# A soft-capped attention with a gated convolution behind it: the order of every engine's work written down in new tables

## The chip, the cores and the metric

The kernel runs on one core of one Trainium2 chip. A core has engines with a queue each: TensorE (PE, matrix products; its weight loads are PEld), VectorE (DVE), ScalarE (ACT), GpSimd (POOL) and SyncE (SP), which here issues all DMAs. Every queue is in order: an instruction that waits holds up all that stand behind it on its engine. The metric is the time of one execution on the device in microseconds (us), the median of several runs; less is better.

## What is computed

```python
def _attn_ref(q, k, v, cap):                       # 8 batches, 12 heads, 448 rows, 64 columns, float32
    scores = np.matmul(q, k.transpose(0, 1, 3, 2)) / np.sqrt(q.shape[-1])
    scores = cap * np.tanh(scores / cap)           # cap = 30
    attn = np.exp(scores - np.max(scores, axis=-1, keepdims=True))
    attn = attn / (np.sum(attn, axis=-1, keepdims=True) + 1e-09)
    return np.matmul(attn, v)

def _moe_ref(x, w_val, conv_w, w_out):             # x: 8 x 448 x 768, the heads side by side
    gate_pre = causal_conv(x, conv_w)              # 5 taps along the rows, each column by itself
    gate = 1.0 / (1.0 + np.exp(-gate_pre))
    return gate * (x @ w_val) @ w_out              # both weights 768 x 768
```

The weights w_val, w_out and conv_w come as float64.

## The kernel before

**Tiles.** The work is cut into 48 *pairs* p: two heads of one batch, which fill 128 partitions. Six pairs make a batch, called a *block* b (0 to 7). Everything is held turned, with a head's columns on the partitions.

For a pair, the steps are, with the lines of the profile: `load_q`, `load_k` (L186), `load_v` (L198): DMAs. `tq`, `tk` (L305): VectorE transposes q and k. `scores` (p, i), i = 0 to 3 (L326): TensorE makes scores of 112 keys against 448 queries for both heads, into a PSUM tile `pss` of which there are two; for pairs 0 to 12 in plain fp32, from pair 13 on in three products of high and low halves, which `q_hi`, `k_hi` (ScalarE, L311) and `q_lo`, `k_lo` (VectorE, L240) make. `tanh` (L334) and `exp` (L338): ScalarE, one tile of 112 x 896 each, into `pt`, of which there are six. `add` (VectorE, L345, L348): for pairs 6 to 10 the four `pt` are added in twos, from pair 11 on to one. `av` (p, i) (L363): TensorE, the product with v, into the one `psa`. `sums` (L375): TensorE, the row sums by a product with ones, into the one `psz`; four rounds for pairs 0 to 5, two up to 10, then one. `turn_sums`, `recip`, `spread`, `mul` (VectorE, L383 to L404): the division, which leaves x in one of two buffers `u`. `x_hi` (ScalarE, L409), `x_lo` (VectorE, L240): the halves of x. `conv` (p, 0 to 4) (L421 to L425): the five taps, on VectorE; for p < 11 the first one on ScalarE.

For a block and each of its six groups d of 128 columns: `sigmoid` (ScalarE, L431), `val` (TensorE, L446 to L448, two halves of nine matmuls, each half over three pairs' x), `gate` (VectorE, L452), `gated_hi` (ScalarE, L455), `gated_lo` (VectorE). Then `out_part` (TensorE, L475 to L477, six or eight tiles m, two halves of nine matmuls each), `store` (ScalarE copies the tile, L483) and `store_out` (DMA, L487); `keep_tail` (GpSimd, L462) carries rows over to the next block. val and out share two PSUM tiles `psf`. In twelve steps the weights are split into halves: `weight_load`, `late_load` (DMA), `weight_first` (ScalarE, L140, L141), `weight_second`, `weight_third` (VectorE).

**Order.** Nothing is ordered by a scheduler. Each step gets a number, "when", in units of pairs: p plus an entry of a table. The list of all steps is sorted by it, and each engine's queue holds its steps in that order:

```python
with tc.manual_schedule(engines={ENG.Activation, ENG.PE, ENG.DVE, ENG.Pool, ENG.SP}):
    for _, _, f, a in sorted(events, key=lambda e: e[:2]):
        f(*a)
```

The numbers are no times: an engine runs its next step as soon as what it needs is there. Before, the tables hold one row for a kind of pair (`EARLY` for pairs 0 to 5, `PAIRED`, `STEADY`, `SPLIT`, with changes like `TOGETHER` or `GATE_FIRST` by p % 6), so that the order repeats from block to block. For pair 25 it gives:

```
TensorE  scores25.0 scores25.1 av24.0-3 sums24 val3.1 (2 halves) scores25.2 scores25.3 val3.2 scores26.0 scores26.1 av25.0-3 sums25
ScalarE  tanh25.0 tanh25.1 exp25.0 exp25.1 q_hi26 k_hi26 sigmoid3.0-5 x_hi24 tanh25.2 gated_hi3.0 gated_hi3.1 tanh25.3 exp25.2 exp25.3
VectorE  add25.0 q_lo26 k_lo26 gate3.0 gate3.1 gated_lo3.0 gated_lo3.1 x_lo24 conv24.0-4 gate3.2 add25.1 add25.2
```

and for pair 27 `x_lo26 conv26.0-4 add27.1 add27.2` on VectorE. All six sigmoids of a block stand together.

Of the kernel before, what the change touches and what calls it, by code (L numbers as in the profile page):

```python
# [40 lines left out]
STEADY = {  # L41
    "load_q": -1.9,
    "load_k": -1.85,
    "load_v": -0.6,
    "tq": -0.90,
    "tk": -0.85,
    "scores": (0.0, 0.05, 0.62, 0.67),
    "tanh": (0.06, 0.13, 0.68, 0.75),
    "exp": (0.22, 0.29, 0.82, 0.89),
    "add": (0.52, 1.03, 1.06),  # L50
    "av": (1.10, 1.15, 1.20, 1.25),
    "sums": (1.28,),
    "turn_sums": 1.41,
    "recip": 1.42,
    "spread": 1.44,
    "mul": 1.50,
    "x_hi": 1.52,
    "x_lo": 1.58,
    "conv": (1.60, 1.61, 1.64, 1.67, 1.70),
}  # L60

SPLIT = STEADY | {"q_hi": -0.69, "k_hi": -0.68, "q_lo": -0.475, "k_lo": -0.47}
PAIRED = STEADY | {"add": (0.52, 1.03), "sums": (1.28, 1.29)}
EARLY = {
    "load_q": -1.9,
    "load_k": -1.85,
    "load_v": -0.7,
    "tq": -0.72,
    "tk": -0.70,
    "scores": (-0.50, -0.49, 0.10, 0.11),  # L70
    "tanh": (0.0, 0.01, 0.35, 0.36),
    "exp": (0.17, 0.18, 0.52, 0.53),
    "av": (0.28, 0.37, 0.65, 0.80),
    "sums": (0.29, 0.38, 0.66, 0.81),
    "turn_sums": 1.02,
    "recip": 1.03,
    "spread": 1.04,
    "mul": 1.05,
    "x_hi": 1.30,
    "x_lo": 1.34,  # L80
    "conv": (1.31, 1.50, 1.52, 1.54, 1.56),
}

SIXTH = PAIRED | {k: EARLY[k] for k in ("tq", "tk", "scores", "tanh", "exp")} | {"add": (0.38, 0.62)}


TOGETHER = {
    "scores": (0.0, 0.05, 0.31, 0.32),
    "tanh": (0.06, 0.13, 0.34, 0.36),
    "exp": (0.22, 0.29, 0.47, 0.53),  # L90
    "add": (0.52, 0.60, 0.61),
}
NEXT_TOGETHER = {
    "turn_sums": 1.41, "recip": 1.42, "spread": 1.43, "mul": 1.44, "x_hi": 1.45, "x_lo": 1.54,
    "conv": (1.58, 2.16, 2.17, 2.18, 2.19),
}
PREPARE_TOGETHER = {"q_hi": -0.69, "k_hi": -0.68, "q_lo": -0.44, "k_lo": -0.43}

GATE_FIRST = {"x_lo": 1.66, "conv": (1.67, 1.68, 1.69, 1.70, 1.71)}
LATE_X = {"x_lo": 1.76, "conv": (1.78, 1.80, 1.83, 1.86, 1.89)}  # L100
NEARLY, NPAIRED, NPLAIN = 6, 11, 13

VAL_FIRST = (6.50, 6.85, 7.36, 7.74, 8.36, 8.74)
VAL = (6.85, 7.36, 7.74, 8.36, 8.74, 9.36)
SIG_FIRST, SIG_AT = 6.92, 7.44
OUT_EVEN = (9.80, 10.36, 10.74, 11.36, 11.74, 12.36)
OUT_ODD = (9.80, 10.36, 10.74, 10.80, 11.36, 11.74, 11.80, 12.36)
OUT_LATE = (9.80, 10.36, 10.74, 11.74, 12.36, 12.60)
PART = 0.13
KEEP_AT = 10.2  # L110
W_AT = (0.70, 1.70, 2.70, 3.70, 4.70, 5.70, 7.1, 8.035, 9.035, 9.7, 10.4, 11.035)
W_LOAD = -0.5
W_SECOND, W_THIRD, W_THIRD_EARLY = 0.02, 0.05, 0.71
W_FREE = 11.3
CW_LOAD, CW_AT = -0.55, 0.6
EPS = 1e-9
# [13 lines left out]
def float64_split(nc, raw, mid, hi, lo, t):  # L130

    tf = t.bitcast(F32)
    top = raw[..., 1].bitcast(F32)

    def first():
        nc.scalar.activation(tf, top, AF.Copy, scale=2.0 ** -112)  # L140
        nc.scalar.sign(top, top)  # L141
# [60 lines left out]
def fast_path(tc, io, u2, q, k, v, w_val, conv_w, w_out, out, capt):  # L202
# [22 lines left out]
    with ExitStack() as ctx:  # L225
# [37 lines left out]
        wstate = {}  # L263
# [11 lines left out]
        def late_load(n):  # L275
# [5 lines left out]
            wstate[n] = wstate[n], shifted(late, NH)  # L281

        def weight_first(n):
            _, c, nh, w = wsteps[n]
            t = wsc.tile([P, WC, NH], I32, name="w_t")
            wstate[n] = float64_split(nc, *wstate[n], w[:, c, nh, 0], w[:, c, nh, 1], t)
# [63 lines left out]
        def bank(p, name):  # L350

            if p < NEARLY and p % 2:
# [3 lines left out]
        def attnv(p, i):  # L356
# [5 lines left out]
            for j, r in enumerate(ROWS):  # L362
                nc.tensor.matmul(  # L363
                    st["o"][r, :S], vloads[p][:, j, i], t[:, j], start=(i == 0), stop=(i == NKT - 1)
                )

        def sums(p, i):

            st = state[p]
            n = len(tables[p]["sums"])  # L370
# [5 lines left out]
            if i == n - 1:  # L376
                vloads.pop(p)
# [29 lines left out]
        def x_hi(p):  # L407
            xh = wk.tile([P, S], F32R, name="xh", bufs=NXX)
            nc.scalar.copy(xh, gates[p][1][:, PAD:PAD + S])  # L409
# [80 lines left out]
        cw_steps = []  # L490
        events = []
        tables = [EARLY if p < NEARLY else SIXTH if p == NEARLY else PAIRED if p < NPAIRED else STEADY if p < NPLAIN else SPLIT for p in range(NP)]
        for p in range(NPAIRED, NP):
            if p % NPAIR == 0:
                tables[p] = tables[p] | LATE_X

        def together(p):
            return NPLAIN < p < NP and p % NPAIR not in (1, 3)

        for p in range(NPLAIN, NP):  # L500
            if together(p - 1):
                tables[p] = tables[p] | PREPARE_TOGETHER
            if together(p):
                tables[p] = tables[p] | TOGETHER
            if p % NPAIR == 2:
                tables[p] = tables[p] | GATE_FIRST
            if together(p + 1):
                tables[p] = tables[p] | NEXT_TOGETHER

# [13 lines left out]
        for p, table in enumerate(tables):  # L523
            for name, f in steps.items():
                x = table.get(name, ())
                if isinstance(x, tuple):
                    for i, y in enumerate(x):
                        at(p + y, f, p, i)
                else:
                    at(p + x, f, p)  # L530
        for b in range(B):
            t0 = NPAIR * b
            for d in range(NCC):
                sig = SIG_AT if b else SIG_FIRST
                y = (VAL if b else VAL_FIRST)[d]
                at(t0 + sig, sigmoid, b, d)
                for i in range(PARTS):
                    at(t0 + y + i * PART, val, b, d, i)
                done = t0 + max(y + PARTS * PART, sig + 0.17)
                at(done + 0.01, gate, b, d)  # L540

                last = d == NCC - 1
                at(done + (0.02 if last else 0.08), gated_hi, b, d)
                at(done + (0.03 if last else 0.12), gated_lo, b, d)
            if b % 2 == 0:
                at(t0 + KEEP_AT, keep_tail)
            for m, y in enumerate(OUT_ODD if b % 2 else OUT_LATE if b == B - 2 else OUT_EVEN):
                for i in range(PARTS):
                    at(t0 + y + i * PART / 2, out_part, b, m, i)
                at(t0 + y + 0.20, store, b, m)  # L550
                at(t0 + y + 0.40, store_out, b, m)
        for n, t0 in enumerate(W_AT):
            third = [x + (W_THIRD if x > NEARLY else W_THIRD_EARLY) for x in W_AT]
# [186 lines left out]
```

## Time and profile before

| | |
|---|---|
| median of 3 runs | 743.75 us (742.98 to 746.29) |
| span of the profiled execution, first to last instruction | 739.6 us |
| TensorE busy | 717.1 us, 97% |
| VectorE busy | 593.0 us, 80% |
| ScalarE busy | 534.7 us, 72% |
| GpSimd busy | 9.0 us, 1% |
| moved by DMA | 63.75 MB |

The profile is of one execution of its own. Busy is the time in which at least one instruction of the engine ran. A row of a timeline is: start, duration, engine, line, operation, tile written <- tiles read, form, count, and in brackets the engine's idle time just before and what ended it. A row of waits is: who waited for whom, total us, times, longest. The end of a matmul is modelled, so that the records of two in a row overlap.

### The profile page before, as it was taken

Reading aid. Unit: us, or ns where it says so; the run is one execution under the profiler, and the core shown is the slowest. Engines: PE = TensorE matmul, PEld = TensorE weight load, DVE = VectorE, ACT = ScalarE, POOL = GpSimd, SP = SyncE. Lnnn points to the kernel's source line nnn. Section 1 sums busy time; section 2 is a strip of 40 time slices with the busy share of each in tenths; the row PEclk is TensorE's granted clock in tenths of the full one; section 3 lists DMA queues with packets and bytes.
Section 4 is the critical chain, followed back from the end, with each engine's and each line's share of the span. In section 5 each row is a group of like instructions: output and inputs, shape, how many; then the busy total and the mean of one; then the engine's idle time right before and its main releaser. Section 6 shows DMA issues by size and latency. Waiting matters only on the chain.

```text
span 739.6 us, 10858 instructions
## 1 busy us (share of the span) xinstructions
PE 717.1 (97%) x3972; PEld 488.8 (66%) x3972; DVE 593.0 (80%) x972; ACT 534.7 (72%) x708; POOL 9.0 (1%) x16
## 2 busy tenths in 40 slices
PE   5999999999999999999999999999999999999997
PEld 2333655556767776686677766757766876676997
DVE  2899999888997789988899669988899778997410
ACT  5899977787876678776957679587787659774311
POOL 0000001000000000000000000000000000000000
PEclk9999999999999999999999999999999999999999
DMA  6998867854223332224331333223322333200001
GB/s 109 223 212 209 202 171 154 225 118 80 39 49 80 74 74 38 61 67 88 57 57 47 88 75 65 39 69 74 73 38 61 70 87 57 51 24 33 23 22 68
DMA packets 241820, 63.75 MB, mean 86 GB/s; under 512 B 228448, under 2 KB 235616, under 8 KB 241760
## 3 DMA queue, kind: packets, MB, share of 16 engines
q1 hardware_dynamic: 241760, 62.98, 38.6%
q8 instruction: 33, 0.54, 0.3%
q14 instruction: 27, 0.22, 0.1%
HBM read 51.94 MB, written 11.01 MB: 85 GB/s over the span
## 4 chain that ended last, share of the span: by engine, by line
PE 52%; DVE 21%; ACT 13%; issue 2%; SPq 1%; DMA 0%; DVEq 0%; ACTq 0%
PE pss L326 9%; PE psf L475 8%; PE psf L477 7%; PE psf L476 7%; DVE gate L425 7%; PE psa L363 6%; PE psf L446 4%; PE psf L447 4%; PE psf L448 4%; ACT pt L334 3%; PE psz L375 3%; DVE pa L348 3%; ACT gate L431 3%; ACT pt L338 2%; DVE pa L345 2%
## 5 line engine op out<-in xcount | busy, mean ns | idle before, releaser
L334 ACT ACTIVATE pt<-pss,rc 112x896 f32<-112x896 f32 x192 | 185.1, 1004 | 39.2 <-PE pss L326 39.2
L338 ACT ACTIVATE pt<-pt,capt 112x896 f32<-112x896 f32 x192 | 189.6, 1041 | 0.1
L363 PE MATMUL psa<-pt,vn 112*64 112x448 f32 x720 | 147.7, 546 | 0.0
L425 DVE SCALAR_TENSOR_TENSOR gate<-u,cw,gate 128x448 f32<-128x448 f32 x192 | 130.6, 680 | 5.7
L475 PE MATMUL psf<-wo,g_h 128*128 128x384 f32 x336 | 115.7, 344 | 0.0
L477 PE MATMUL psf<-wo,g_l 128*128 128x384 f32 x336 | 112.6, 335 | 0.0
L476 PE MATMUL psf<-wo,g_h 128*128 128x384 f32 x336 | 112.4, 335 | 0.0
L446 PE MATMUL psf<-xh,wv 128*128 128x448 f32 x288 | 107.5, 373 | 0.1
L448 PE MATMUL psf<-xl,wv 128*128 128x448 f32 x288 | 104.5, 363 | 0.0
L447 PE MATMUL psf<-xh,wv 128*128 128x448 f32 x288 | 104.4, 362 | 0.0
L363 PEld LDWEIGHTS psa<-pt,vn 112*64 112x64 f32 x720 | 47.8, 136 | 81.4 <-issue 69.7
L348 DVE TENSOR_TENSOR pa<-pt 112x896 f32<-112x896 f32 x84 | 91.1, 1085 | 2.8 <-ACT pt L338 2.8
L483 ACT COPY osb<-psf 128x384 f32<-128x384 f32 x56 | 26.6, 475 | 65.3 <-PE psf L477 63.6
L383 DVE STREAM_TRANSPOSE zt<-psz 128x448 f32<-128x448 f32 x45 | 28.8, 640 | 54.2 <-PE psz L375 54.2
L475 PEld LDWEIGHTS psf<-wo,g_h 128*128 128x128 f32 x336 | 63.1, 188 | 12.3 <-issue 11.3
L446 PEld LDWEIGHTS psf<-xh,wv 128*128 128x128 f32 x288 | 54.0, 187 | 20.2 <-issue 5.4
L476 PEld LDWEIGHTS psf<-wo,g_h 128*128 128x128 f32 x336 | 63.1, 188 | 0.0
L477 PEld LDWEIGHTS psf<-wo,g_l 128*128 128x128 f32 x336 | 63.1, 188 | 0.0
L326 PE MATMUL pss<-qt,kt 64*112 64x448 f32 x208 | 49.6, 594 | 12.3 <-DVE guard L249 7.8
L455 ACT CAST g_h<-gate 128x448 fp32r<-128x448 f32 x48 | 26.3, 562 | 47.2 <-DVE gate L452 47.0
L326 PE MATMUL pss<-qh,kh 64*112 64x448 f32 x280 | 58.0, 408 | 0.0
L409 ACT CAST xh<-u 128x448 fp32r<-128x448 f32 x48 | 27.1, 566 | 42.3 <-DVE u L404 42.0
(74 smaller groups left out, 908.6 us busy)
## 6 DMA issues: line engine op xcount, KB each, us to landing
vn<-in_v_dram SPq DMA_DIRECT2D x96, 112.0 KB, 2.6
out_dram<-osb SPq DMA_DIRECT2D x56, 192.0 KB, 1.9
qn<-in_q_dram SPq DMA_DIRECT2D x188, 56.0 KB, 2.5
kn<-in_k_dram SPq DMA_DIRECT2D x188, 56.0 KB, 2.4
w_raw<-in_moe_w_val_dram SPq DMA_DIRECT2D x12, 384.0 KB, 5.1
w_late<-in_moe_w_val_dram SPq DMA_DIRECT2D x12, 384.0 KB, 4.4
w_raw<-in_moe_w_out_dram SPq DMA_DIRECT2D x12, 384.0 KB, 3.8
w_late<-in_moe_w_out_dram SPq DMA_DIRECT2D x12, 384.0 KB, 4.8
```

Of the source, the lines that this page charges most:

```text
L326: nc.tensor.matmul(ps[:CH, j, :S], st[x][r, c], st[y][r], start=(n == 0), stop=(n == len(parts) - 1))
L334: nc.scalar.activation(st["p", i], st.pop(("s", i)), AF.Tanh, scale=rc8[:CH])
L338: nc.scalar.activation(t, t, AF.Exp, scale=capt[:CH])
L348: nc.vector.tensor_tensor(st["a", i], st["p", 2 * i], st["p", 2 * i + 1], op=ALU.add)
L363: nc.tensor.matmul(st["o"][r, :S], vloads[p][:, j, i], t[:, j], start=(i == 0), stop=(i == NKT - 1))
L425: nc.vector.scalar_tensor_tensor(g, u[:, i:i + S], cw[:, hp, i:i + 1], g, ALU.mult, ALU.add)
L446: nc.tensor.matmul(o, w_h, xh, start=(c == 0), stop=False)
L447: nc.tensor.matmul(o, w_l, xh, start=False, stop=False)
L448: nc.tensor.matmul(o, w_h, xl, start=False, stop=(c == NCC - 1))
L475: nc.tensor.matmul(o, g_h[:, d, s], w_h, start=(d == 0), stop=False)
L476: nc.tensor.matmul(o, g_h[:, d, s], w_l, start=False, stop=False)
L477: nc.tensor.matmul(o, g_l[:, d, s], w_h, start=False, stop=(d == NCC - 1))
```

## The change

The rows by kind of pair give way to explicit tables: `PAIRS` with a row of its own for every pair (41 entries, one for each step in the order of `STEPS`, "-" where a pair has no such step), `BLOCKS` with a row for every block (for each d: sigmoid, two halves of val, gate, gated_hi, gated_lo; for each m: two halves of out_part, store, store_out; then keep_tail) and `WEIGHTS` with a row for every weight step. Every entry is its own number. The tiles, buffers, shapes and the number of rounds of sums and adds stay.

```diff
-STEADY = {
-    "load_q": -1.9,
...
-VAL = (6.85, 7.36, 7.74, 8.36, 8.74, 9.36)
-SIG_FIRST, SIG_AT = 6.92, 7.44
...
-W_AT = (0.70, 1.70, 2.70, 3.70, 4.70, 5.70, 7.1, 8.035, 9.035, 9.7, 10.4, 11.035)
...
+STEPS = (
+    "load_q load_k load_v tq tk q_hi k_hi q_lo k_lo scores scores scores scores tanh tanh tanh tanh exp exp exp exp "
+    "add add add av av av av sums sums sums sums turn_sums recip spread mul x_hi x_lo conv conv conv conv conv"
+).split()
+PAIRS = """
...
+-2.755 -1.548 0.688 -2.289 -1.481 -1.594 -0.947 -1.309 -0.372 -0.21 -0.236 0.313 0.244 -0.12 0.033 0.445 0.478 0.478
+  0.7 0.779 1.041 1.144 1.179 1.232 0.992 1.021 1.146 1.246 1.455 - - - 1.462 1.48 1.528 1.724 2.379 2.648 2.404 2.517
+  2.861 2.934 3.075
...
+WEIGHTS = """
+-4.855 -1.763 -2.156 -1.27 -0.233
+0.802 1.523 1.156 1.227 2.293
+2.154 2.964 2.861 2.935 3.223
+3.016 3.564 3.703 3.854 4.003
+4.19 4.977 5.204 5.319 5.9
+5.564 6.372 6.246 6.423 6.673
...
+        for p, row in enumerate(pairs):
+            seen = {}
+            for name, when in zip(STEPS, row):
+                i = seen[name] = seen.get(name, -1) + 1
+                if when is not None:
+                    at(p + when, steps[name], p, *([i] if STEPS.count(name) > 1 else []))
+        for b, row in enumerate(plan(BLOCKS)):
+            t0, row = NPAIR * b, iter(row)
+            for d in range(NCC):
+                at(t0 + next(row), sigmoid, b, d)
+                for i in range(PARTS):
+                    at(t0 + next(row), val, b, d, i)
+                for f in (gate, gated_hi, gated_lo):
+                    at(t0 + next(row), f, b, d)
```

(The row of `PAIRS` shown is that of pair 32.) Small edits let the steps of a tile come in another order than before: `x_hi` and `x_lo` read `u2[p % 2]` and not the tile that conv notes, the late half of a weight is looked up when the third weight step runs, and v is given up with the last `av` and not with the last `sums`.

Sorted, the new numbers give for pair 32, in the stretch from its first tile of scores to its sums and on ScalarE and VectorE in the stretches that the prediction speaks of:

```
TensorE  scores32.2, then val4.4 and val4.3 in halves, scores33.0 scores33.1 av32.0 av32.1 av32.2 av32.3 sums32
ScalarE  tanh32.2 q_hi33 tanh32.3 exp32.0 gated_hi4.2 exp32.1 exp32.2 q_hi34 gated_hi4.1 x_hi30 exp32.3
VectorE  add32.1 conv31.1 tq35 add32.2
```

for pair 35:

```
ScalarE  tanh35.0 tanh35.1 k_hi36 exp35.0 q_hi36 store4.2 tanh35.2 exp35.1 tanh35.3 sigmoid5.2 exp35.2 exp35.3
TensorE  scores35.0 av34.0 av34.1 av34.2 sums34 av34.3 scores35.2 scores35.3 out4.3 and out4.4 in halves scores36.0 scores36.1 av35.0 av35.1 av35.2 sums35 av35.3
```

and around weight step 9:

```
TensorE  scores9.0 scores9.3, out0.2 and out0.1 in halves, scores10.1 scores10.0 av9.0 av9.1 sums9.0 scores10.3 scores10.2 av9.2 sums9.1 av9.3 scores11.0
ScalarE  tanh9.0 gated_hi0.5 weight_first9 exp9.1 exp9.0 tanh9.3 exp9.3 store0.2 tanh10.1 tanh10.0 weight_first10 store0.1 tanh10.2 tanh10.3
```

The sigmoids of a block stand in three to five places among the tanhs and exps of several pairs.

More of the change, by code (lines that the diff above doesn't have):

```diff
@@ L38 @@
 NPT = 6
-STEADY = {
-    "load_q": -1.9,
[L43 to L97, printed above, removed]
@@ new lines, with plan @@
+7.475 7.712 7.865 7.932 8.599
+8.032 8.912 8.606 8.81 9.094
+9.156 9.712 9.45 9.646 9.848
+10.01 10.445 10.217 10.425 10.731
+10.475 11.217 10.992 11.363 11.754
+"""
+CW_LOAD, CW_AT, W_FREE = -1.043, 0.208, 11.768
+NPAIRED, NPLAIN = 11, 13
+BANKED = 6
+EPS = 1e-9
+def plan(text):
+    rows = []
+    for line in text.strip("\n").split("\n"):
+        cells = [None if x == "-" else float(x) for x in line.split()]
+        if line.startswith(" "):
+            rows[-1] += cells
+        else:
+            rows.append(cells)
+    return rows
@@ L262, in fast_path @@
         ]
-        wstate = {}
+        wstate, wlate = {}, {}
         gated = {i: cpool.tile([P, NCC, GW], F32R, name=f"g_{i}") for i in "hl"}
@@ L280, in late_load @@
                 nc.sync.dma_start(late[:, i, 1:1 + 4 * NH], w[r:r + P, nh * NH:(nh + 1) * NH].bitcast(U16))
-            wstate[n] = wstate[n], shifted(late, NH)
+            wlate[n] = shifted(late, NH)
         def weight_first(n):
@@ L350, in bank @@
         def bank(p, name):
-            if p < NEARLY and p % 2:
+            if p < BANKED and p % 2:
                 return ps_f.tile([P, 512], F32, name="psf")
@@ L365, in attnv @@
                 )
+            if i == NKT - 1:
+                vloads.pop(p)
         def sums(p, i):
             st = state[p]
-            n = len(tables[p]["sums"])
+            n = rounds[p]
             if i == 0:
@@ L413, in x_lo @@
             xl = wk.tile([P, S], F32R, name="xl", bufs=NXX)
-            less(nc.vector, xl, gates[p][1][:, PAD:PAD + S], xs[p])
+            less(nc.vector, xl, u2[p % 2][:, PAD:], xs[p])
             xs[p] = xs[p], xl
@@ L490, in fast_path @@
         cw_steps = []
+        pairs = plan(PAIRS)
+        rounds = [sum(x is not None for n, x in zip(STEPS, row) if n == "sums") for row in pairs]
         events = []
[L492 to L508, printed above, removed]
         def at(when, f, *a):
@@ L522, in fast_path @@
         )
[L523 to L532, printed above, removed]
+        for p, row in enumerate(pairs):
[4 more added lines that the diff above has]
+                    at(p + when, steps[name], p, *([i] if STEPS.count(name) > 1 else []))
@@ L542, in fast_path @@
-                last = d == NCC - 1
-                at(done + (0.02 if last else 0.08), gated_hi, b, d)
-                at(done + (0.03 if last else 0.12), gated_lo, b, d)
-            if b % 2 == 0:
[L546 to L551, printed above, removed]
@@ new lines, in fast_path @@
+            for m in range(2 * (NT + b % 2)):
+                for i in range(PARTS):
+                    at(t0 + next(row), out_part, b, m, i)
+                at(t0 + next(row), store, b, m)
+                at(t0 + next(row), store_out, b, m)
+            if b % 2 == 0:
+                at(t0 + next(row), keep_tail)
+        for n, row in enumerate(plan(WEIGHTS)):
+            for f, when in zip((weight_load, late_load, weight_first, weight_second, weight_third), row):
+                at(when, f, n)
```

179 lines of the change are left out of this document (147 added, 32 removed), and 32 rows, old and new, of the table BLOCKS.

## The prediction

> **What bounds the kernel now.** I read the page first, then TensorE's waits, then the stages.
>
> ```profile
> span 739.6 us, 10858 instructions
> ...
> PE 717.1 (97%) x3972; PEld 488.8 (66%) x3972; DVE 593.0 (80%) x972; ACT 534.7 (72%) x708; POOL 9.0 (1%) x16
> ...
> PEclk9999999999999999999999999999999999999999
> ```
>
> TensorE is idle for 739.6 - 717.1 = 22.5 us and its granted clock stays in the top tenth. TensorE's own rows in the view of waits say where most of the idle time lies:
>
> ```profile
> PE pss L326 <- DVE guard L249: 7.8, 1, 7.8
> PE pss L326 <- ACT pt L334: 4.4, 6, 1.6
> PE psz L375 <- DVE pa L345: 3.5, 9, 0.6
> PE psf L363 <- DMA vn<-in_v_dram: 1.2, 1, 1.2
> ```
>
> The columns are the total, the times and the longest. 7.8 us is the start, before the first scores, where the order of q, k and the constants stays as it was. The rest of 22.5 - 16.9 = 5.6 us is nearly all the end, after the last matmul. Between them TensorE loses only 4.4 + 3.5 + 1.2 = 9.1 us. The stages (busy us of each engine):
>
> ```profile
> 0.00:75.00 75.00, 64.68 (x300) 22.10 (x300) 55.40 (x104) 63.77 (x76) 0.66 (x8) 1.00 0.86 188
> ...
> 185.00:666.00 481.00, 477.15 (x2759) 340.69 (x2759) 411.97 (x668) 359.94 (x482) 5.19 (x6) 1.00 0.30 62
> ```
>
> Columns: width, TensorE, weight load, VectorE, ScalarE, GpSimd, clock, DMA share. In the long middle ScalarE works 360 of 481 us (75%), VectorE 412 (86%), TensorE 477 (99%). TensorE bounds it. Only in the first 75 us is ScalarE nearly as full.
>
> A busy TensorE is not always a dense one, so I looked at where its matmuls start:
>
> ```profile
> 301.41 0.36 PE L447 MATMUL psf<-xh,wv 128*128 128x448 f32 x1
> 301.61 0.37 PE L448 MATMUL psf<-xl,wv 128*128 128x448 f32 x1
> 301.90 0.46 PE L326 MATMUL pss<-qh,kh 64*112 64x448 f32 x2
> 302.20 0.36 PE L326 MATMUL pss<-ql,kh 64*112 64x448 f32 x2
> 302.40 0.37 PE L326 MATMUL pss<-qh,kl 64*112 64x448 f32 x2
> ```
>
> The values and the scores run one (or one pair) per 0.20 us. At the change of shape the steps are 0.29 and 0.30: a change between the three shapes (scores 64*112, av and sums 112*64, val and out 128*128) costs 0.09 + 0.10 = 0.19 us without any wait.
>
> **The change.** No operation is added to TensorE, VectorE or the DMA queue. To see what moves I sorted the old and the new tables by their numbers into each engine's order and counted.
>
> *Shape changes.* The old order has 208 of them, the new one 198. 10 x 0.19 = -1.9 us.
>
> *Scores waiting for tanh, the 4.4 us.* The two longest of the six:
>
> ```profile
> 128.17 1.01 PE L326 MATMUL pss<-qt,kt 64*112 64x448 f32 x4 [1.45 <-ACT pt L334]
> 130.78 1.01 PE L326 MATMUL pss<-qt,kt 64*112 64x448 f32 x4 [1.61 <-ACT pt L334]
> ```
>
> ```profile
> 126.08 0.57 ACT L409 CAST xh<-u 128x448 fp32r<-128x448 f32 x1 [3.17 <-DVE u L404]
> 126.56 0.66 ACT L421 ACTIVATE gate<-u,cw 128x448 f32<-128x448 f32 x1
> 127.13 0.99 ACT L334 ACTIVATE pt<-pss,rc 112x896 f32<-112x896 f32 x1
> 128.02 0.89 ACT L140 ACTIVATE w_t<-w_raw 128x768 f32<-128x768 f32 x1
> 128.94 0.90 ACT L141 ACTIVATE w_raw<-w_raw 128x768 f32<-128x768 f32 x1
> 129.74 0.99 ACT L334 ACTIVATE pt<-pss,rc 112x896 f32<-112x896 f32 x1
> ```
>
> Scores have two banks, so the first two tiles of pair 10 wait for the last two tanhs of pair 9. Ahead of these ScalarE waits 3.17 us for x of pair 8 (its queue is in order), and between them it runs weight step 9, 1.7 us from 128.02 to 129.74. In the new order x_hi of pair 8 stands behind a tanh of pair 12. Weight step 9 still stands between two tanhs, but the second tile of pair 10 has 6.5 us of out steps (36 matmuls, one per 0.18) and two tiles of scores (1.01 for the one at 128.17) as cover against tanh, cast, weight step, two exp and tanh, 0.96 + 0.55 + 1.7 + 1.98 + 0.96 = 6.2 us (prices below). I take both waits as gone: -3.1. The other four, 4.4 - 3.1 = 1.3 us, fall in the first 75 us, where ScalarE is full. Up to the first tanh of pair 6 the old order gives it 6 weight steps, 5 casts x_hi and 5 conv copies; the new one 5, 3 and 4. That relieves it of 1.7 + 2 x 0.57 + 0.66 = 3.5 us, more than the 1.3: -1.3. The weight step that left runs in pair 6 or 7 beside val. If that cover fails, its 1.7 us come back.
>
> *The wait for v, 1.2 us.* Pair 1's v is queued behind a conv load, two weight loads and q, k of pair 2. In the new order it stands ahead of k2, the late weight half and the conv load, but behind q2 and the first weight load; between 0 and -1.2 I take -0.6. Elsewhere I looked at what stands ahead of each v load in the DMA queue: always over 6 us of TensorE's work lie between the last store or av that it must await and the av that reads it, against 2.6 us to landing:
>
> ```profile
> vn<-in_v_dram SPq DMA_DIRECT2D x96, 112.0 KB, 2.6
> ```
>
> The moved q, k and weight loads and the GpSimd step have such cover too; bound: one wait like this, +1.2.
>
> *Sums waiting for adds, the 3.5 us.* They have two causes. The first is ScalarE's burst once a block:
>
> ```profile
> 178.68 0.55 ACT L311 CAST qh<-qt 128x448 fp32r<-128x448 f32 x1
> 179.13 0.57 ACT L311 CAST kh<-kt 128x448 fp32r<-128x448 f32 x1
> 179.72 1.28 ACT L431 ACT_TABLE_LOAD   x1
> 181.01 2.92 ACT L431 ACTIVATE gate<-gate 128x448 f32<-128x448 f32 x6
> ...
> 184.29 1.00 ACT L334 ACTIVATE pt<-pss,rc 112x896 f32<-112x896 f32 x1
> ...
> 187.14 1.28 ACT L338 ACT_TABLE_LOAD   x1
> ```
>
> Six sigmoids between two table loads, 5.5 us, in the midst of pairs 13, 19, 25 ... 43. (tanh at 184.29 needs no load after sigmoid; exp does.) The second is VectorE in pairs 15, 21, 27 ... 45, where five convs stand ahead of the last two adds:
>
> ```profile
> 307.61 2.13 DVE L425 SCALAR_TENSOR_TENSOR gate<-u,cw,gate 128x448 f32<-128x448 f32 x3
> 309.65 1.09 DVE L348 TENSOR_TENSOR pa<-pt 112x896 f32<-112x896 f32 x1
> 310.77 1.09 DVE L345 TENSOR_TENSOR pa<-pa,pa 112x896 f32<-112x896 f32 x1
> ```
>
> ```profile
> 311.92 0.97 PE L375 MATMUL psz<-pa,ones 112*64 112x448 f32 x4 [0.62 <-DVE pa L345]
> ```
>
> The new order has at most two convs among those adds and spreads the sigmoids, so both causes go. But it pays in two ways. It breaks 8 groups of sigmoids into 31, and the tables change between exp and sigmoid 61 times in place of 15: 46 loads x 1.28 = 59 us more on ScalarE. And it often puts sums before the last one or two av, which takes 0.8 to 1.6 us of cover from the adds.
>
> The cost I worked out pair by pair. For each of the pairs 13 to 47 the chain from a tile of scores through ScalarE's queue up to the last exp and VectorE's queue up to the last add is set against TensorE's work between that tile and sums. Prices:
>
> ```profile
> L334 ACT ACTIVATE pt<-pss,rc 112x896 f32<-112x896 f32 x192 | 185.1, 1004 | 39.2 <-PE pss L326 39.2
> L338 ACT ACTIVATE pt<-pt,capt 112x896 f32<-112x896 f32 x192 | 189.6, 1041 | 0.1
> ...
> L305 DVE STREAM_TRANSPOSE qt<-qn 128x448 f32<-128x448 f32 x47 | 29.9, 637 | 2.5 <-DMA qn<-in_q_dram 2.5
> ```
>
> ```profile
> 320.59 0.18 PE psf L477
> 320.77 1.40 PE pss L326 x12
> 322.17 3.16 PE psa L363 x16
> ```
>
> A tanh is 185.1/192 = 0.96, an exp 0.99. Pair 32, the worst of the new order: from scores32.2 on ScalarE runs 2 tanh, 4 exp, 5 casts and a load, 1.92 + 3.96 + 2.75 + 1.28 = 9.9 us; VectorE adds 2 x 1.09, a conv of 0.71 and a transpose of 0.64, 3.5; together 13.4. TensorE has four half val steps (36 x 0.20 = 7.2), two tiles of scores (1.4) and four av (3.2), 11.8. Short by 1.6. Pairs 26 and 35 are short by 1.2 each, pairs 16, 21, 23, 24, 33, 39 and 41 by up to 0.5; with pair 32 some 5.7 us. The same working for the old order gives 0.2 to 0.45 for pairs 13, 19 ... 43, where the trace shows:
>
> ```profile
> 366.89 0.97 PE L375 MATMUL psz<-pa,ones 112*64 112x448 f32 x4 [0.30 <-DVE pa L345]
> ```
>
> So the method finds a wait of this size. An idle reading understates it, since a matmul's record of 0.54 us is followed after 3.16/8 = 0.39 by the next when nothing waits: 9 x 0.15 = 1.4 on top of 3.5. Old waits -4.9, new ones +5.7, net +0.8; between -4.9 and, as rival 1 has it, +15.6.
>
> **A rule that speaks against the change.** In these rows a switch of tables takes the 1.28 us of the load and no more: the cast before it ends at 179.70 and the load starts at 179.72, sigmoid at 181.01. The Trainium skill ("ScalarE: Activation LUTs", sections "What ACT_TABLE_LOAD costs" and "Table sets: the hidden batching unit") asks to batch calls by table set and puts a switch at 2.66 us, with a drain of 1.38 behind the load. By that price, an estimate from the page, the 46 switches would be 122 us, and ScalarE would be full in the middle. The trace agrees with the load's 1.28 and shows no drain; the sum goes by the trace.
>
> **Sum**, against the profiled execution: -1.9 - 3.1 - 1.3 - 0.6 + 0.8 = -6.1, so 739.6 - 6.1 = 733.5 us of span. The median of the runs, 743.75, is 4.15 above the span; left as it is, that gives **737.6 us**.
>
> **Rivals.** *1. ScalarE's loads reach TensorE (slower).* The blocks of the middle get 42 of the 46 loads, 54 us: ScalarE goes from 360 to 414 of 481 us, 86%. My working starts each pair with ScalarE's queue empty. 16 of the 35 pairs have less than 1.3 us to spare or are short; if ScalarE comes to their first tanh one load late, each loses 1.28 more: 20.5 in place of 5.7, or 14.8 on top, 752.4 us. It decides when ScalarE's backlog at the first tanh of a pair passes about 1 us. For it: two loads and a sigmoid were enough to move sums in the old order. Against: ScalarE waited 39.2 us for scores, so it usually is early.
>
> *2. The gains come back (no change).* VectorE or ScalarE, with work now interleaved at other places, makes new waits of the old size in the first 185 us (3.1 + 1.3 + 0.6 come back): 742.6 us. For it: in the first 75 us the DMA share is 0.86 and ScalarE stays at about TensorE's pace. Against: less work stands in that stage.
>
> *3. All waits for adds vanish (faster).* The chains overlap better than the working allows: 5.7 less, 731.9 us.
>
> *4. The change does not keep the operations.* The sorted tables hold the same steps as before (q and k of pair 0 were loaded outside them already); only the table loads differ, and they are in the sum.
>
> **How the numbers follow.** 0.5%, 3.7 us, is what a measurement of this kernel can tell from no change: the bounds are 740.0 and 747.5. Forecast 0.45, rival 3 0.10 (both faster), rival 2 0.22, rival 1 0.20, a mishap of another queue 0.03. So faster 0.55, same 0.22, slower 0.23. The range reaches from rival 3, 731.9, to rival 1, 752.4; what lies outside is a forecast that is better still or a rival 1 with more pairs. Of the forecast alone it would be 732 to 741.
>
> **What would show it.** In the new profile: about 62 table loads of 1.28 us and ScalarE busy near 594 us; TensorE's row for scores behind tanh under 1.5 us; the row for sums behind adds at about the old 3.5, now in pairs 26, 32 and 35 and not once a block. Wrong is the forecast if TensorE's idle time between start and end passes 15 us, above all behind exp or adds in the middle, or if new waits in the first 185 us equal the old.

## The result, and the profile after

| | us, median | lowest to highest | runs |
|---|---|---|---|
| before | 745.02 | 742.98 to 746.3 | 4 |
| after | 738.36 | 737.59 to 739.93 | 4 |
| before, beside the second measurement | 742.61 | 740.85 to 745.2 | 16 |
| after, measured a second time (new_again) | 736.21 | 735.39 to 737.61 | 4 |

The ratio on record is 0.9926 (95% interval 0.9898 to 0.9954), and 0.9902 (0.9876 to 0.9928) the second time. By the medians the changed kernel is faster by 6.7 and 6.4 us, where 6.1 was forecast. The size came out. The sum behind it did not, as the rows below show. One run of before (1424 us, recorded clock 1.0, cause unknown) and one of the experiment old_spread (1181 us, mean clock 0.56, the one that was profiled) are left out of every comparison here.

The page of the kernel after, the lines that answer to those shown of before:

```profile
span 738.0 us, 10918 instructions
...
PE 713.9 (97%) x3972; PEld 488.4 (66%) x3972; DVE 569.6 (77%) x972; ACT 598.4 (81%) x754; POOL 6.0 (1%) x16
...
PEclk9999999999999999999999999999999999999999
```

Two differences can be read from it. TensorE's busy time fell from 717.1 to 713.9 us, by 3.2. Its idle time is 738.0 - 713.9 = 24.1 us; before it was 22.5. The profile of the second measurement has a span of 735.7 us and again 713.9 busy, so 21.8 idle. The new order has taken hardly any waiting time away. What it did is to move it, as TensorE's waits after say (total, times, longest):

```profile
PE pss L466 <- DVE guard L389: 8.0, 1, 8.0
PE psz L517 <- DVE pa L485: 2.2, 3, 0.8
PE psz L517 <- ACT pt L478: 1.8, 2, 1.4
PE pss L466 <- ACT pt L474: 1.7, 3, 0.8
PE psa L503 <- DMA vn<-in_v_dram: 1.4, 1, 1.4
PE psf L503 <- DMA vn<-in_v_dram: 1.1, 1, 1.1
PE psz L517 <- DVE pa L488: 0.9, 1, 0.9
PE psf L517 <- ACT pt L478: 0.7, 1, 0.7
```

Scores behind tanh went from 4.4 to 1.7, sums behind adds from 3.5 to 2.2 + 0.9. New are sums behind exp (1.8 + 0.7). The wait for the v of pair 1 (1.2 before) is gone, and two others for v have come, of pair 0 (1.4) and of pair 5 (1.1). The stages, in the columns of before, and ahead of them the row of before for the second one:

```profile
75.00:185.00 110.00, 106.80 (x540) 65.65 (x538) 99.13 (x160) 89.38 (x117) 3.14 (x2) 1.00 0.66 158
```

```profile
0.00:75.00 75.00, 60.39 (x278) 19.82 (x280) 44.83 (x89) 59.55 (x70) 0.66 (x8) 1.00 0.79 173
75.00:185.00 110.00, 108.92 (x558) 67.39 (x560) 101.88 (x171) 97.23 (x123) 1.03 (x2) 1.00 0.69 161
185.00:666.00 481.00, 478.06 (x2778) 342.75 (x2776) 395.89 (x670) 419.44 (x527) 4.35 (x6) 1.00 0.31 63
```

In the first 75 us TensorE works 60.4 us in place of 64.7 and so does ScalarE less, 59.6 in place of 63.8: both wait. In the second stage TensorE works 108.9 us in place of 106.8. In the middle ScalarE works 419 us (forecast 414), 87%, and TensorE is still as full as before (478 to 477). The table loads are there in the number that was forecast, 31 + 30 and one at the start:

```profile
L571 ACT ACT_TABLE_LOAD x31 | 39.8, 1283 | 0.5
L478 ACT ACT_TABLE_LOAD x30 | 38.5, 1283 | 0.5
```

For a finer account I took the times from one matmul's start to the next in the trace, less the usual step, and added those above 0.15 us, stage by stage (0 to 75, 75 to 185, 185 to 430, from 430 on; sum; the wait for the constants at the start is not in them):

| kernel | 0-75 | 75-185 | 185-430 | from 430 | sum |
|---|---|---|---|---|---|
| before | 5.0 | 3.4 | 2.7 | 3.1 | 14.1 |
| after | 8.6 | 1.2 | 1.5 | 3.1 | 14.4 |
| after, second profile | 8.1 | 0.6 | 1.5 | 3.0 | 13.2 |

About 2.5 us are gained in the second stage and 1.2 behind it, and 3.1 to 3.6 lost in the first. The loss is not the same in every execution: three kernels below (new_first, new_grouped, new_sums_last) keep TensorE's new order in that stage, and the same account of their profiles gives 6.9, 6.2 and 5.4 us there. So the new start loses between 0.4 and 3.6 us, and the two profiles of the changed kernel are the two worst of five.

By the profiles the changed kernel is faster by 1.6 to 3.9 us. That understates it: of its four runs each time, the profiled one was the longest (739.93 and 737.61 us). Where the rest of the 6.4 to 6.7 comes from is the matter of the first experiments.

### The profile page after: what moved, and what is told of

It is laid out like the page before. It is cut to its first block, busy times and chain, and to the rows that moved or that the text cites. A ratio compares the mean times of both kernels' runs of the same rounds, so it can differ in the third digit from the quotient of the medians.

```text
span 738.0 us, 10918 instructions
## 1 busy us (share of the span) xinstructions
PE 713.9 (97%) x3972; PEld 488.4 (66%) x3972; DVE 569.6 (77%) x972; ACT 598.4 (81%) x754; POOL 6.0 (1%) x16
## 4 chain that ended last, share of the span: by engine, by line
PE 67%; ACT 12%; DVE 4%; issue 1%; DMA 1%; SPq 0%; DVEq 0%; ACTq 0%
PE psa L503 13%; PE pss L466 12%; PE psf L615 7%; PE psf L617 7%; PE psf L616 7%; PE psf L586 6%; PE psf L587 5%; PE psf L588 5%; ACT pt L478 4%; PE psz L517 4%; ACT pt L474 3%; ACT L478 2%; DVE pa L488 1%; DVE pa L485 1%; ACT g_h L595 1%
## 5 line engine op out<-in xcount | busy, mean ns | idle before, releaser
L474 ACT ACTIVATE pt<-pss,rc 112x896 f32<-112x896 f32 x192 | 188.2, 1003 | 59.3 <-PE pss L466 51.0
L478 ACT ACTIVATE pt<-pt,capt 112x896 f32<-112x896 f32 x192 | 195.0, 1041 | 1.1
L503 PE MATMUL psa<-pt,vn 112*64 112x448 f32 x720 | 150.9, 545 | 1.6 <-DMA vn<-in_v_dram 1.4
L565 DVE SCALAR_TENSOR_TENSOR gate<-u,cw,gate 128x448 f32<-128x448 f32 x192 | 126.6, 671 | 0.9
L586 PEld LDWEIGHTS psf<-xh,wv 128*128 128x128 f32 x288 | 54.0, 187 | 11.8 <-issue 4.2
L466 PE MATMUL pss<-qt,kt 64*112 64x448 f32 x208 | 48.0, 578 | 9.5 <-DVE guard L389 8.0
L588 PEld LDWEIGHTS psf<-xl,wv 128*128 128x128 f32 x288 | 54.0, 187 | 3.7
L587 PEld LDWEIGHTS psf<-xh,wv 128*128 128x128 f32 x288 | 54.1, 188 | 3.1
L466 PE MATMUL pss<-qh,kl 64*112 64x448 f32 x280 | 51.5, 362 | 0.0
L466 PE MATMUL pss<-ql,kh 64*112 64x448 f32 x280 | 51.5, 362 | 0.0
```

The source lines that it names most:

```text
L466: nc.tensor.matmul(ps[:CH, j, :S], st[x][r, c], st[y][r], start=(n == 0), stop=(n == len(parts) - 1))
L474: nc.scalar.activation(st["p", i], st.pop(("s", i)), AF.Tanh, scale=rc8[:CH])
L478: nc.scalar.activation(t, t, AF.Exp, scale=capt[:CH])
L503: nc.tensor.matmul(st["o"][r, :S], vloads[p][:, j, i], t[:, j], start=(i == 0), stop=(i == NKT - 1))
L565: nc.vector.scalar_tensor_tensor(g, u[:, i:i + S], cw[:, hp, i:i + 1], g, ALU.mult, ALU.add)
L586: nc.tensor.matmul(o, w_h, xh, start=(c == 0), stop=False)
```

## The experiments

Theory T: the order alone is what acts; TensorE gains by fewer shape changes and fewer waits, and ScalarE's added loads lie where it has room. Rival R1: the loads reach TensorE. R2: a wait that is taken away makes the next step late. The kernels with "old" keep the order of before (but for three or four neighbouring steps near the weight steps 6 and 7, which change places), those with "new" the changed one; all are written as tables in the form of the changed kernel, so their lines are shifted (scores L349, tanh L357, exp L361, adds L368 and L371, av L386, sums L400, x_hi L432, sigmoid L454, gated_hi L478, out L498 to L500, store L506). In the edits, "x9.2" is tile 2 of pair 9, "sigmoid2.4" step 4 of block 2.

### old_tables: the changed code, the old numbers

```diff
 PAIRS, BLOCKS, WEIGHTS
-  numbers of the new order
+  numbers that give the old order
```

> The changed code with the old order written into the new tables, so that only the small edits beside the tables are tried, and the old order gets a second profile. If the order makes the whole difference (my theory): the time of the kernel before, 745.0 us, within 0.3%, and 15 loads of ScalarE's tables. If the edits themselves gain (rival): about 738.4, the time of the changed kernel. The second profile tells whether the 739.6 us of the first was a typical span or a short one: the runs after the change lie 1.9 us above their spans, so by that 743 us is expected.

Measured: 742.93 us (740.65 to 744.39), ratio 0.9988 (0.9968 to 1.0008). The small edits beside the tables do nothing that can be measured; what acts is the order. The trace shows one thing more. TensorE's timeline, with what it waited for in brackets:

```profile
127.75 1.01 PE L349 MATMUL pss<-qt,kt 64*112 64x448 f32 x4 [1.39 <-ACT pt L357]
130.37 1.40 PE L349 MATMUL pss<-qt,kt 64*112 64x448 f32 x4 [1.61 <-ACT pt L357]
131.70 3.73 PE L386 MATMUL psa<-pt,vn 112*64 112x448 f32 x12
```

The same two waits as in the profile of before. But the scores at 130.37 take 1.40 us and not 1.01, and the av behind them are drawn out too (3.73 us for 12; 3.23 for 16 elsewhere). The stretches of that time, the granted clock third from the right:

```profile
126.00:130.90 4.90, 1.90 (x11) 0.59 (x9) 4.70 (x8) 4.87 (x7) 0.00 (x0) 1.00 0.78 133
130.90:134.30 3.40, 3.40 (x12) 1.00 (x10) 3.37 (x6) 3.40 (x6) 0.00 (x0) 0.50 0.52 158
```

For 3.4 us behind the second wait the clock is 0.50. The profile of before had the waits without this, which is why the prediction has no such term. That it happens in many runs of the old order is seen in their mean clocks. Of 68 runs of before that stand beside these experiments, 29 have a mean clock of 0.998 or more and a median of 741.4 us, 16 have 0.996 or 0.997 and 742.7 us, and 23 have less and 745.2 us. One stretch of 3.4 us at half the clock takes 1.7/740 = 0.0023 off the mean. The eight runs of the changed kernel all have 0.998 or more, and their median is 737.6 us. So runs of like clock differ by 741.4 - 737.6 = 3.8 us. This puts together runs of several series. In the second measurement alone, 8 of the 16 runs of before have 0.998 or more and a median of 741.5, against 736.2: 5.3 us. So some 1 to 3 us of the gain go with a clock that falls less often; the split is not known better.

### new_first and old_first: half of each

The tables of one order up to the sums of pair 12, those of the other behind.

```diff
-  old order throughout
+  new_first: new order up to sums12, old order behind
+  old_first: old order up to sums12, new order behind
```

> The new order up to the sums of pair 12, the old order from there on (207 changes of shape on TensorE, 21 table loads). My prediction put 5.0 us of gain into the first 185 us: 740 us. What the two profiles show of waits there (first 75 us: 5.0 before, 8.6 after; next 110 us: 3.4 before, 1.2 after) speaks for none, +1.5: 746 us. If ScalarE's loads cost (rival), this kernel, which has few, should beat the changed one: under 737 us.

> The old order up to the sums of pair 12, the new order from there on (199 changes of shape, 57 table loads). By my prediction's terms: 9 changes of shape less, -1.7, and +0.8 for sums: 744 us. By the waits of the two profiles in the middle (5.8 before, 4.6 after): -1.7 - 1.2, 742 us. If the gain lies in this part alone (rival to the prediction's terms): 738 us or less. If the 42 more loads reach TensorE: over 748 us.

Measured: new_first 743.06 (0.9983 to 1.0029 of before), between what the terms and what the waits gave, and old_first 740.44 (0.993 to 0.9978), below both. With its 57 loads it is far from the 748 us of the rival. The gains, 0 and 3, don't add up to the whole 6.4 to 6.7. The trace of new_first says why for one of them: at the seam the old steps meet a ScalarE that the new ones left later, and the sums of pair 13 wait.

```profile
194.19 1.45 PE L400 MATMUL psz<-pa,ones 112*64 112x448 f32 x4 [2.02 <-DVE pa L368]
195.58 0.71 PE L349 MATMUL pss<-qh,kh 64*112 64x448 f32 x2
196.09 0.58 PE L349 MATMUL pss<-ql,kh 64*112 64x448 f32 x2
```

Four sums take 1.45 us (0.97 elsewhere) and the pairs of scores start every 0.37 us (0.20 elsewhere): the clock is 0.52 for 3.4 us again, behind a single wait. A cut through the order makes its own wait, so the halves can't be priced by such cuts to a microsecond. old_first shows the clock's share by itself. Its 12 runs fall into six with a mean clock of 1.0 (738.49 to 739.89 us, median 739.3) and six with 0.992 to 0.995 (741.0 to 744.52, median 743.1): the same program, 3.7 us apart, with the clock.

### old_spread and old_between: the new spread of the sigmoids in the old order

Six sigmoids stand together in the old order. In old_spread they stand in five places, in old_between in three, between pairs, after an exp and before a tanh. Block 2 on ScalarE:

```diff
-  ... q_hi20 k_hi20 sigmoid2.0 to sigmoid2.5 x_hi18 tanh19.2 ...
+  old_spread:  sigmoid2.0 and 2.1 stay; exp19.2 sigmoid2.2 exp19.3; exp20.2 sigmoid2.3 exp20.3; sigmoid2.4 tanh21.0; k_hi22 sigmoid2.5 x_hi20
+  old_between: exp18.3 store1.7 sigmoid2.0 sigmoid2.1 tanh19.0; exp19.3 sigmoid2.2 sigmoid2.3 tanh20.0; exp20.3 gated_hi2.3 sigmoid2.4 sigmoid2.5 tanh21.0
```

> The old order with one thing alone of the new one: the sigmoids of a block stand in five places, each ahead of its gate, in place of one (71 table loads in place of 15, 72 us more on ScalarE; all else as before). My theory: ScalarE has room for the loads, and the six waits of sums behind the burst, 2.7 us, go: 742 us. Rival, loads reach TensorE: of the 56 new loads a fourth on a short chain, 14 x 1.28 = 18 us: 763 us; 745 would mean that both cancel.

> The old order with the sigmoids in three places a block, each behind the last exp of a pair and ahead of the next tanh (43 table loads in place of 15; in the kernel with five places, two of which stood between two exps of one pair, 71 loads). Theory: a load costs only where the chain from scores to sums has no room; here 28 loads, 36 us of ScalarE, cost nothing or gain the six waits behind the burst, 2.7 us: 741 to 743.4 us. Rival, every added group of loads costs as in the kernel with five places (59 us for 28 groups, 2.1 each): 14 groups, 773 us.

Measured: old_spread 802.6 us, ratio 1.079 (1.0758 to 1.0822); old_between 770.95 us, 1.0359 (1.0335 to 1.0384). The only profile of old_spread is that of the 1181 us, so where its 59 us went can't be read from rows. Its other six runs have mean clocks of 0.966 to 0.973; 0.03 x 800 = 24 us, an estimate, is what a lower clock can account for. For old_between the page and the waits have it:

```profile
span 770.3 us, 10893 instructions
...
PE 728.6 (95%) x3972; PEld 491.5 (64%) x3972; DVE 594.4 (77%) x972; ACT 573.4 (74%) x736; POOL 7.8 (1%) x16
```

```profile
PE psf L498 <- ACT g_h L478: 11.3, 6, 1.9
...
PE psz L400 <- DVE pa L368: 6.9, 10, 1.3
PE pss L349 <- ACT pt L357: 6.8, 9, 1.6
PE psf L386 <- DMA vn<-in_v_dram: 2.5, 1, 2.5
PE psz L400 <- DVE pa L371: 1.0, 2, 0.5
```

and of VectorE's waits:

```profile
DVE gate L475 <- ACT gate L454: 13.6, 11, 2.7
```

TensorE's waits are 28.5 us, 19.4 more than the 9.1 of before. The busy time is 728.6 - 717.1 = 11.5 more, with the clock at half in five places of 3.4 us, which give 8.5 of it at most. 19.4 + 11.5 = 30.9, against 770.3 - 739.6 = 30.7 of span: nearly the whole loss is waits and the clock behind them. The largest row is new: out waits six times, once in each of six blocks and up to 1.9 us, for gated_hi. VectorE's row is new too: eleven gates wait for a sigmoid, which now comes up to one and a half pairs later, and what stands behind them on VectorE comes later, in block 1 the gate that out needs among it.

T had the loads free between pairs, and that fell. R1's condition fell with it: ScalarE is 74% busy here and 81% in the changed kernel, which is faster by 35 us. How full ScalarE is does not decide; where the sigmoids and their loads stand does. How much of the loss is the loads, and how much the later sigmoids, these two kernels don't separate, since they change both.

### old_x8: the two waits near 128 us taken away in the old order

```diff
 ScalarE:
-  exp9.1 x_hi8 conv8.0 tanh9.2 weight_first9 tanh9.3 exp9.2
+  exp9.1 tanh9.2 tanh9.3 weight_first9 x_hi8 conv8.0 exp9.2
 VectorE:
-  add9.0 x_lo8 conv8.1 conv8.2 conv8.3 conv8.4 weight_second9 weight_third9 add9.1
+  add9.0 weight_second9 x_lo8 conv8.1 conv8.2 conv8.3 conv8.4 weight_third9 add9.1
```

> The old order with three ScalarE steps moved: x_hi and the first conv of pair 8 and weight step 9 stand behind the last tanh of pair 9 and not ahead of it or between. That takes away what makes TensorE wait twice near 128 us. If the two waits and the clock behind them are a cause (theory): -3.2 and, in the runs in which the clock fell there, another 1.5 to 2: about 739 us against 743.4, mean clock 0.997 or more. If the two waits are filled by others at once (rival): 743 us.

Measured: 742.53 us, 0.9996 (0.9979 to 1.0012). The two waits are gone, and this stands in their place, for an add:

```profile
132.27 0.92 PE L400 MATMUL psz<-pa,ones 112*64 112x448 f32 x4
135.73 1.41 PE L400 MATMUL psz<-pa,ones 112*64 112x448 f32 x4 [2.53 <-DVE pa L371]
137.07 0.69 PE L498 MATMUL psf<-wo,g_h 128*128 128x384 f32 x1
```

2.53 us of one wait for 1.45 + 1.61 of two, and the clock halves behind it. VectorE's rows ahead of that add:

```profile
129.90 2.84 DVE L448 SCALAR_TENSOR_TENSOR gate<-u,cw,gate 128x448 f32<-128x448 f32 x4
...
134.59 1.08 DVE L371 TENSOR_TENSOR pa<-pt 112x896 f32<-112x896 f32 x1
```

VectorE works without a gap from the division of pair 8 to this add: an add, x_lo, four convs and the weight step stand ahead of it, in both orders. The add starts 13.7 us behind the start of the sums of pair 8 here and 13.6 in old_tables, so the moved steps of ScalarE did not touch it. R2 held: VectorE was late as well, the waits for tanh had covered it, and its next reader pays.

### old_convs: the middle's waits for adds taken away in the old order

In the pairs 15, 21, 27 ... 45 the last two adds are put ahead of four of the five convs.

```diff
 VectorE:
-  x_lo14 conv14.0 conv14.1 conv14.2 conv14.3 conv14.4 add15.1 add15.2
+  x_lo14 conv14.0 add15.1 add15.2 conv14.1 conv14.2 conv14.3 conv14.4
```

> The old order with one thing moved on VectorE: in pairs 15, 21, 27, 33, 39 and 45 the last four convs of the pair before stand behind the adds and not ahead of them. My prediction named them as the cause of six waits of sums, 0.23 to 0.79 us each, 3.1 in all. Theory: these six rows are gone and the time is 3 us less, 0.996 of before. Rival (another step is late next, as with the three ScalarE steps of pairs 8 and 9): rows gone, time the same.

Measured: 744.97 us, 1.0024 (1.0006 to 1.0042). The six sums of these pairs wait no more, and the row for sums falls to half. Out waits instead, in blocks 1, 3 and 5:

```profile
PE psf L498 <- ACT osb L506: 4.4, 3, 1.5
PE psz L400 <- DVE pa L368: 1.7, 6, 0.3
```

1.8 us were taken away and 4.4 came. ScalarE's timeline ahead of the first of the three shows the way from the adds to the store:

```profile
224.71 0.57 ACT L334 CAST qh<-qt 128x448 fp32r<-128x448 f32 x1 [1.56 <-DVE qt L328]
225.24 0.57 ACT L334 CAST kh<-kt 128x448 fp32r<-128x448 f32 x1
...
230.01 0.46 ACT L506 COPY osb<-psf 128x384 f32<-128x384 f32 x1
```

The cast of q waits 1.56 us for VectorE's turn of q. The same steps stand ahead of that turn as before, but VectorE now idles in front of the first of the two adds, since the exp is not there yet:

```profile
219.15 1.09 DVE L371 TENSOR_TENSOR pa<-pt 112x896 f32<-112x896 f32 x1 [2.15 <-ACT pt L361]
```

In the old order four convs filled that time. The store that frees a bank for out stands in ScalarE's queue behind that cast and comes later with it. R2 held a second time.

### old_start: the old order for the first six pairs alone

The profiles after have lost 3.1 to 3.6 us in the first 75 us; so the old steps up to the sums of pair 5 were put ahead of the new order.

```diff
-  new order throughout
+  old order up to sums5, new order behind
```

> The old order up to the sums of pair 5, the new one from there on (194 changes of shape, 61 loads). The first 75 us of the new order lose 8.6 us in waits against 5.0 of the old. Theory (stages add up): 3.6 us less than the changed kernel, about 0.988 of the time before, 734.5 us. Rival (the seam costs what the start gains, or the lag of the new start is made up later): 738 us or more.

Measured: 735.41 us (734.47 to 737.09), 0.9893 (0.9872 to 0.9913). From new_again's 736.21 in the same series it can't be told apart. It has 61 loads and 194 shape changes, and the early waits changed by less than hoped, since v of pair 1 comes late here:

```profile
PE psf L386 <- DMA vn<-in_v_dram: 2.7, 1, 2.7
```

The clock halves behind this wait as well.

### new_grouped: 30 fewer loads in the new order

Sigmoids of a block that stood apart are put together, as far as the convs ahead of them and the gates behind them allow. Block 2:

```diff
 ScalarE:
-  exp17.1 sigmoid2.0 x_hi15 ...; store1.1 sigmoid2.1 tanh16.3 ...; k_hi20 sigmoid2.3 sigmoid2.2 sigmoid2.4 exp19.0
+  tanh18.2 exp18.2 sigmoid2.1 sigmoid2.0 sigmoid2.3 sigmoid2.2 sigmoid2.4 store1.7 tanh19.0
```

> The changed order with the sigmoids drawn together as far as convs and gates allow: 31 table loads in place of 61, 38 us less on ScalarE; all else as it was. Theory: the loads of the changed order lie where ScalarE has room, and fewer of them gain at most the waits of sums in pairs 13, 26, 32 and 35, 3 us: 733 to 736 us, 0.987 to 0.990 of before. Rival 1 of the prediction: a third or more of the 30 loads reaches TensorE, then 13 us less: under 725. Third case: a sigmoid that stands later holds up its gate and the out steps, as in the old order with three places: over 745.

Measured: 738.07 us (736.62 to 740.91), 0.994 (0.992 to 0.996). ScalarE is relieved of 40 us:

```profile
PE 714.8 (97%) x3972; PEld 490.3 (67%) x3972; DVE 569.9 (77%) x972; ACT 558.3 (76%) x724; POOL 6.0 (1%) x16
```

and nothing is gained. The waits of sums in the pairs 13, 26, 32 and 35, some 2.3 us together, did go. What grouping brought instead is waits in the pairs 31 (0.9 us) and 36, the longest, 2.5 us, in this row, with half the clock for 3.4 us behind it:

```profile
PE psz L400 <- DVE pa L368: 3.5, 2, 2.5
```

Without these two waits and the clock, 0.9 + 2.5 + 1.7 us, the kernel could be faster by as much, an estimate. So the 30 loads, 40 us of ScalarE, weigh some 5 us at the most: T holds in the main, and that they weigh nothing is not shown, since grouping takes loads away and moves sigmoids at once.

### new_sums_last: sums behind the last av

```diff
 TensorE, in the pairs from 11 on where it stood earlier:
-  av15.0 av15.1 sums15 av15.2 av15.3
+  av15.0 av15.1 av15.2 av15.3 sums15
```

(Pair 15 for example; where sums stood ahead of one av, three or all four it is the same. Some turns of the sums on VectorE stand a little later with them.)

> The changed order with sums behind the last av in all pairs from 11 on. My prediction counted an early sums as 0.8 to 1.6 us of lost cover. The rows of the changed kernel show it in pairs 35 and 41 alone, 1.0 us in all: by the prediction's reason 735 us, by the rows no change that can be measured. Rival: the early sums free their bank and start the division early; behind av the next pair waits: 739 us or more.

Measured: 735.52 us (734.47 to 736.91), 0.9897 (0.9866 to 0.9927), no difference from new_again's 0.9902 that can be measured. The waits in the pairs 35 and 41 went, that in pair 13 fell from 0.97 to 0.31, that in 32 stayed at 0.94.

### best: the waits that were found, taken away one by one

old_start, with the load of v1 earlier and three steps of ScalarE behind the exp that sums wait for.

```diff
 SP:
-  weight_load0 late_load0 load_q2 load_k2 load_v1
+  weight_load0 load_v1 late_load0 load_q2 load_k2
 ScalarE:
-  tanh13.3 sigmoid1.4 k_hi15 ... exp13.3 tanh14.1
+  tanh13.3 k_hi15 ... exp13.3 sigmoid1.4 tanh14.1
-  gated_hi4.1 x_hi30 exp32.3
+  gated_hi4.1 exp32.3 x_hi30
-  tanh35.3 sigmoid5.2 exp35.2 exp35.3
+  tanh35.3 exp35.2 exp35.3 sigmoid5.2
```

> The old order up to the sums of pair 5 and the new one behind it (735.4 us, 0.989 of before), with four steps moved: the v load of pair 1 ahead of the second half of the first weights, one sigmoid out of the exps of pair 13 and one out of those of pair 35, and the cast x_hi of pair 30 behind the exps of pair 32. Theory (each wait has its own step): the wait for v, 2.8 us and the half clock behind it, 1.3, goes, and of the waits in pairs 13, 32 and 35, 2.7 us together, about 2: 729.5 us, 0.981. Rival: others are late next: 734 to 735.

Measured: 733.88 us (731.55 to 734.24), 0.9864 (0.9833 to 0.9894). All its runs lie below the lowest of the eight of the changed kernel, which were not measured beside it, and below the lowest of new_sums_last, which was. Its waits:

```profile
PE pss L349 <- ACT pt L357: 4.0, 9, 1.0
PE psz L400 <- DVE pa L371: 0.9, 1, 0.9
PE psf L498 <- ACT osb L506: 0.8, 1, 0.8
```

The waits for v and the sums of 13 and 35 are gone, pair 32's went from 0.94 to 0.59, no clock halves on the way, and the mean clock of its six runs is 0.999 or 1.0. Against the 729.5 hoped for, the rest came back as scores behind tanh and one wait for a store. It beats the kernel before clearly, and the changed one by a little: the intervals of their ratios overlap.

## Why the prediction was right in its size, and where its sum failed

By its own signs the mechanism is wrong in one part: it named "new waits in the first 185 us" that "equal the old" as a sign against it, and in both profiles of the changed kernel these came. That the median was met so closely is luck, as the last terms show.

- **The bound.** Right. TensorE is busy 97% after as before.
- **Shape changes, -1.9.** Agrees in sign and order: 10 fewer, and busy time 717.1 to 713.9, -3.2. Of the other 1.3 some 0.9 are chance: at the start the matmuls of scores follow each other every 0.74 us in place of 0.46, up to 13.4 us in the profile before and up to 11.0 after, and in all the profiles that moment lies between 10.6 and 13.6, in either order.
- **The two waits near 128, -3.1.** The waits are gone (the second stage has 0.6 to 1.2 us of waits where 3.4 were). The step left out what follows such waits in other runs: 3.4 us at half the clock. That missing term is most likely the larger part of the 1 to 3 us that go with the clock. The profiles of old_tables and old_first show it at this place; where the clock falls in the other runs wasn't seen, since only one execution of each is recorded.
- **The four early waits, -1.3.** Failed, with the wrong sign: the first 75 us have 3.1 to 3.6 us more in the profiles of the changed kernel, 0.4 to 1.9 in the three others with this start. The working counted ScalarE's load, and the weight step that left. It did not follow the wait of weight step 1 for its own load. In the DMA queue that load stood right behind v1; now k2, k3, the late half of weight 0, the conv load, q3, k5 and v2 come between. The step, at 29.49 before and without a wait, stops ScalarE's queue:

```profile
38.33 0.93 ACT L279 ACTIVATE w_t<-w_raw 128x768 f32<-128x768 f32 x1 [3.38 <-DMA w_raw<-in_moe_w_val_dram]
```

  Behind it stand the last tanh and two of the exps of pair 2, and TensorE's rows there are these:

```profile
41.17 1.91 PE L466 MATMUL pss<-qt,kt 64*112 64x448 f32 x8 [0.69 <-ACT pt L474]
43.56 0.97 PE L517 MATMUL psz<-pt,ones 112*64 112x448 f32 x4 [0.48 <-ACT pt L478]
45.89 0.97 PE L517 MATMUL psz<-pt,ones 112*64 112x448 f32 x4 [1.36 <-ACT pt L478]
```

- **The waits for v, -0.6.** The wait that was named is gone, -1.2. But the step that called all other loads covered failed: v of pair 0 (+1.4, its av now starts one tile of scores earlier) and v of pair 5 (+1.1) wait, together twice the bound of one such wait. In new_first, new_grouped and new_sums_last the waits for v are 0.4 to 1.0 us in all, so their size is a matter of the execution.
- **Sums, +0.8.** Too dark. Waits from 185 us on fell from 5.8 to 4.6. Of the pairs that were named, 32 waits 0.94 (forecast 1.6), 35 0.8 (1.2), 26 0.27 (1.2) and 41 0.2 (up to 0.5): the places right, the sizes a fifth to two thirds, most likely since each chain was set against TensorE with all of it in series. Pair 13, 0.97, was missed. That early sums cost cover shows in the waits of 35 and 41, 1.0 us, which go in new_sums_last, but not in a time that can be measured.
- **The time around the span, 4.15.** Failed. A run lies 1.7 to 2.0 us above its own span. By that the profiled execution of before took about 741.4 us, an estimate: a short one, below the four runs shown, and the difference of 4.15 was most likely its luck with the clock. The forecast of 733.5 for the span met 735.7 and 738.0, and 737.6 for the median was met because the sum was 2.2 to 4.5 us too good and the offset 2.3 too large: two errors that cancelled.
- **Rival 1, the loads.** Did not happen: 62 loads came, and new_grouped shows that 30 of them weigh some 5 us at the most, where the rival had 14.8. The mechanism is real where the order has no room, as old_spread and old_between show.
- **Rival 2, gains come back in the first 185 us.** Half right: of waits, 8.4 us before and 8.7 to 9.8 after. By the profiles alone it is what happened there, and the shape changes, the middle and the clock made the gain.
- **The table rule.** The loads are 1.283 us each in every kernel here; no drain is seen behind one. By the price in the Trainium skill ("ScalarE: Activation LUTs", section "What ACT_TABLE_LOAD costs"), an estimate, 30 fewer switches would free 80 us of ScalarE; it was 598.4 - 558.3 = 40.1.

What stays open: the share of loads and of later sigmoids in the loss of old_between and old_spread; how the gain divides between waits and clock; and why the new start loses 0.4 us in one execution and 3.6 in another.

## What to carry to other kernels

In queues that are in order, a wait shows which chain is late and not which step to move: follow the chain to the next reader before counting the wait as gain, and follow a moved step's own wait, not only its duration. Extra work on an engine with idle time can be nearly free or dear, by its place. Judge a small change by runs of like clock, and hold the profiled run against the spread of the others before adding to its span.

## What the runs showed of the hardware

The clock halves behind shorter waits than I had thought possible: 3.4 us at 0.50 to 0.52 behind waits of 1.9 us (old_between, two of six), 2.0 us (new_first), 2.5 us (old_x8, new_grouped) and 2.7 us (old_start), and behind two of 1.4 and 1.6 us within 4 us (old_tables, old_first); the like two waits in before and old_convs did nothing. Behind 2.70 us in old_first it lasted longer, the mean clock of 6.9 us being 0.51:

```profile
25.30:32.20 6.90, 6.11 (x16) 3.34 (x16) 6.67 (x11) 5.48 (x7) 0.00 (x0) 0.51 0.83 190
```

A halving costs about 1.7 us on top of its wait (half of 3.4, an estimate), and waits up to 1.6 us that stand alone have none in these profiles. The Trainium skill ("TensorE: Matmul & The Clock Gate", section "HAM oscillation — how this bites in real kernels") puts the fall at idle gaps above about 3.4 us. The length of the throttled stretch agrees with its window of about 3.4 us; the gap does not, and the measurement decides.

What decides can be read from the traces together. In each of them the recorded clock changes only at whole multiples of 3.413 us after its first entry, and that entry lies 10.6 to 13.6 us behind the start of the span, at another place in each execution. Cut into these stretches, the thirteen profiles other than that of old_spread show TensorE idle for 1.8 to 2.5 us in the twelve stretches after which the clock goes from full to half, up to its last matmul, and for 1.86 us at most in those after which it stays; the two ranges overlap by less than 0.1 us. The pair of waits near 128 us falls into two stretches in before, with 1.70 and 1.36 us, and lies with 1.92 us in one in old_tables. So in these traces the idle time within one stretch counts and not the length of a wait, and where a stretch begins is the chance of the execution.
